# First loads of a gated attention and GEGLU kernel: one DMA queue in the order of need, wk in finer pieces, seven warm-up matmuls

## The chip, the cores and the metric

The kernel runs on one core of a Trainium2 chip. The core has five engines that run side by side, each with its own in-order stream of instructions: TensorE (PE in the profile; its weight loads are shown apart as PEld), VectorE (DVE), ScalarE (ACT), GpSimd (POOL) and SyncE (SP). They wait for each other through semaphores. Loads from device memory are issued by SP or ACT, each into a queue of its own (q1 and q10 in the profile), and moved by 16 DMA engines. The metric is the device time of one execution in microseconds (us), given as the median over several runs.

## The reference

The input x has 2048 rows of 512. Two branches are computed from it and mixed by a gate for each row. Branch a is attention with a compressive memory, 32 heads of 16, in 4 segments of 512 rows; branch b is a GEGLU feed-forward with an inner width of 1792.

```python
g = sigmoid((x * gate_w).sum(-1, keepdims=True))
# branch a, for each segment s of 4:
p = softmax(qs @ ks.T * scale + causal_mask); a_dot = p @ vs
pq = phi(qs); a_mem = (pq @ M) / (pq @ z + 1e-6)
o = sigmoid(beta) * a_mem + (1 - sigmoid(beta)) * a_dot
M = M + phi(ks).T @ vs; z = z + phi(ks).sum()
a = concat(o) @ wo
# branch b
b = (gelu(x @ w_gate) * (x @ w_up)) @ w_down
return g * a + (1 - g) * b
```

## The kernel before

The work is cut by segment s = 0 to 3. For each segment the kernel makes K and Q transposed (tasks `K{s}_t`, `Q{s}_t`, t = 0 to 3, each four matmul steps kb over the contraction), V by tiles of 128 rows (`V{s}_t`), the scores (`qk{s}_{t}{A0,B0,L,A1,B1}`, L868), their exponentials on ScalarE (`exp...`, L874), the causal masks on GpSimd (`msk...`, L877), the products with V (`pv...`, L916 and L924), the memory (`mz`, `num`), the gate and up projections of the feed-forward (`G{s}_ft`, `U{s}_ft`, ft = 0 to 13) and the last projection with `wo` and `w_down` (`D{s}_t`). Nearly all plain matmuls are recorded at L505, which is a helper.

The order on each engine is written out by hand in the table `ORDER` (L41 to L138): one list of task names for each of `pe`, `act`, `dve`, `pool` and `sp`. A name with a dot is a piece of a task: `Q0_1.2` is the part of Q0_1 that starts at contraction step 2. In segment 0 the K tasks are cut finer: each step is made in two halves of 256 rows, so that `K0_t.0` to `K0_t.3` are the steps kb = 0 to 3 of rows 0 to 255, and `K0_t.4` to `K0_t.7` those of rows 256 to 511. The class `Sched` (L207 on) walks these lists to give out the four rotating PSUM banks `psW` and the order of planning; `DMA_RATE`, `COLD`, `LANDING` and the like are its assumptions. They decide nothing else: the engines run as the lists and the semaphores have it.

The scores of one group fill `psXALL`, four banks, and ScalarE turns them into one `pt` tile (128x2048) per group. The next group of scores can't be written before that exponential has read the banks. So PE is given other work between two groups: the pieces of G, U, V, K, Q and D that stand between two `qk` names in the list. Where that work is shorter than the exponential, PE waits.

What happens first (L562 to L607):

- SP and ACT both issue loads at the start. SP issues `x0_0` and `x0_1` (rows 0 to 255 and 256 to 511 of x, 256 KB each, into the tile `hT` of the other buffer, L572), then `w_wv0`, `w_wv1` (256 KB each), `w_wg0` (896 KB), and then, mixed with the small loads `w_gwb` and `w_beta`, the four transposing loads `x1_0` to `x1_3` of segment 1 (L553), and `w_wg1`. ACT issues `w_wk0`, `w_wk1`, `w_wq0`, `w_wq1` (256 KB each); `wk{0,1}` hold the contraction steps 0-1 and 2-3.
- PE runs warm-up matmuls on a constant (L590): ten before the first real work and an eleventh, `warm10`, after the first eight transposes. They compute nothing that is used.
- When `x0_0` has landed, PE transposes rows 0 to 255 of x against an identity (L599, eight transposes into `psXALL`, tasks `x0t0a_0`, `x0t0b_0`, `x0t1_0`); DVE and ACT copy them to the tile `xT` (L607, L606, tasks `x0ev...`); then K of the first half is made, step by step.
- On ScalarE the activation table is loaded by the first activation, `tload` (L567), which stands behind the four loads that ACT issues.
- GpSimd makes the identity, masks (L609 to L613), small constants (L621, L622) and then fills the V tiles (L616, L618).

From the score group `qk0_0A0` on, the attention of segment 0 runs, with V0, Q1, K1, V1 and the G tasks of segments 0 and 1 as the work between the groups. In the list of before the first task that reads segment 1 of x is `G1_1.0`, just ahead of `qk0_0B0`.

Of the kernel before, what the change touches and what calls it, by code (L numbers as in the profile page):

```python
# [32 lines left out]
COLD = 4.9  # L33
# [4 lines left out]
    "w_wk0": 4.8, "x0_0": 4.4, "w_wk1": 6.2, "x0_1": 5.8, "w_wq0": 8.2, "w_wv0": 7.4, "w_wq1": 10.1, "w_wv1": 8.9,  # L38
    "w_wg0": 11.5, "x1_0": 12.1, "w_gwb": 12.4, "x1_1": 13.0, "w_beta": 13.3, "x1_2": 13.8, "x1_3": 14.3,
# [39 lines left out]
        "U3_9.0 U3_9.2 U2_2.0 U2_2.2 U3_8.0 U3_7.0 qk3_0B0 U3_5.0 U3_10.0 U3_8.2 U3_7.2 U3_5.2 qk3_0L U3_10.2 "
        "U3_3.0 U3_3.2 U3_4.0 D2_0.0 qk3_0A1 num3_01.0 U3_4.2 D2_0.2 D2_0.4 num3_00.0 D2_0.6 num3_02.0 qk3_0B1 "  # L80
        "D2_0.8 D2_0.10 D2_1.0 D2_1.2 U3_6.0 qk3_1A0 D2_0.12 U3_2.0 D2_0.14 U3_6.2 U3_2.2 qk3_1B0 D2_0.16 D2_1.4 "
        "U3_13.0 D2_1.6 D2_1.8 qk3_1A1 num3_11.0 num3_10.0 D2_1.10 D2_1.12 D2_1.14 U3_13.2 qk3_1B1 U3_1.0 "
        "num3_12.0 D2_1.16 U3_1.2 U3_0.0 qk3_2A0 pv3_0_0 pv3_0_1 U3_0.2 D2_3.0 qk3_2B0 D2_3.2 D2_3.4 pv3_1_1 "
        "pv3_1_0 qk3_2L D2_3.6 D2_3.8 D2_3.10 D2_2.0 D2_3.12 qk3_2A1 D2_3.14 D2_2.2 D2_2.4 D2_2.6 D2_3.16 qk3_2B1 "
        "D3_1.0 D2_2.8 D2_2.10 U3_12.0 U3_12.2 qk3_3A0 D3_1.2 D2_2.12 U3_11.0 D3_1.4 D2_2.14 qk3_3B0 U3_11.2 "
        "D3_0.0 D3_1.6 D2_2.16 D3_0.2 qk3_3A1 pv3_2_0 pv3_2_1 D3_1.8 D3_0.4 qk3_3B1 D3_0.6 D3_1.10 D3_0.8 D3_1.12 "
        "D3_0.10 D3_3w1.0 pv3_3_0 pv3_3_1 D3_3w0.0 D3_0.12 D3_2.0 D3_2.2 D3_0.14 D3_2.4 D3_2.6 D3_1.14 D3_0.16 "
        "D3_1.16 D3_3w1.4 D3_3w1.8 D3_3w0.4 D3_3w1.12 D3_3a1.0 D3_2.8 D3_2.10 D3_2.12 D3_2.14 D3_2.16 D3_3w0.8 "
        "D3_3w0.12 D3_3a0.0 "),
    "act": (  # L90
        "w_wk0 w_wk1 w_wq0 w_wq1 tload x0ev0b_0 x0ev1_0 K0_1ev K0_0even pke0_0 Q0_1ev Q0_0ev Q0_3ev gexp Vev0_1 "
        "exp0_0A0 Vev0_3 Vev0_0 exp0_0B0 gsum0_1 exp0_0L Gev1_1 exp0_0A1 gexs0 Gev0_3 exp0_0B1 pke0_1 exp0_1A0 "
        "Gev1_0 exp0_1B0 Q1_0ev exp0_1A1 pqe1_0 Gev1_9 exp0_1B1 K1_1ev Gev0_9 exp0_2A0 K1_2ev exp0_2B0 pqe1_1 "
        "exp0_2L K1_3ev exp0_2A1 Gev1_12 exp0_2B1 gsum1_0 exp0_3A0 Vev1_3 exp0_3B0 Gev1_3 exp0_3A1 Gev0_12 gexs1 "
        "exp0_3B1 gelu0_0 Gev1_13 gelu0_2 gelu0_6 gelu0_10 gelu1_0 gelu1_7 exp1_0A0 kl1_01 exp1_0B0 exp1_0L "
        "Q2_1ev exp1_0A1 exp1_0B1 pke1_0 exp1_1A0 pke1_1 exp1_1B0 fin0_0 exp1_1A1 pqe2_0 exp1_1B1 fin0_2 exp1_2A0 "
        "K2_0ev exp1_2B0 pqe2_1 exp1_2L exp1_2A1 exp1_2B1 gsum2_0 exp1_3A0 gsum2_2 exp1_3B0 gexs2 Q3_1ev exp1_3A1 "
        "K2_2ev exp1_3B1 gelu2_0 gelu2_1 gelu2_2 gelu2_3 gelu2_4 gelu2_5 gelu2_6 gelu2_7 gelu2_8 gelu2_9 gelu2_10 "
        "gelu2_11 gelu2_12 gelu2_13 exp2_0A0 exp2_0B0 pke2_0 exp2_0L exp2_0A1 pke2_1 exp2_0B1 fin1_0 exp2_1A0 "
        "Q3_3ev exp2_1B0 fin1_2 exp2_1A1 exp2_1B1 Vev3_0 exp2_2A0 exp2_2B0 pqe3_0 exp2_2L exp2_2A1 K3_3ev "  # L100
        "exp2_2B1 exp2_3A0 exp2_3B0 gsum3_3 gexs3 exp2_3A1 pqe3_1 exp2_3B1 gelu3_0 gelu3_1 gelu3_2 gelu3_3 "
        "gelu3_4 gelu3_5 gelu3_6 gelu3_7 gelu3_8 gelu3_9 gelu3_10 gelu3_11 gelu3_12 gelu3_13 exp3_0A0 exp3_0B0 "
        "exp3_0L exp3_0A1 exp3_0B1 exp3_1A0 exp3_1B0 exp3_1A1 exp3_1B1 exp3_2A0 exp3_2B0 exp3_2L exp3_2A1 "
        "exp3_2B1 fin2_3 exp3_3A0 exp3_3B0 exp3_3A1 exp3_3B1 fin3_0 fin3_1 fin3_2 fin3_30 "),
# [1079 lines left out]
```

## Time and profile before

| | us |
|---|---|
| median of 3 runs | 266.92 (266.64 to 267.32) |
| time of the profiled execution | 267.31 |
| its span, first to last instruction | 265.6 |
| PE busy in it | 261.7 |
| DVE, ACT, POOL busy | 201.2, 209.8, 109.0 |

The profile is of one execution. Its span is from the first to the last instruction; the time of the same execution is 1.7 us longer. TensorE is the busiest engine by far, and the table of slices on the page shows it busy in nine tenths or more of every slice but the first and the last.

### The profile page before, as it was taken

The page shows a single profiled execution, that of the slowest core. Times are in us where ns is not written, and L with a number is a line of the kernel's source. Part 1 is how long each engine was busy: PE and PEld are TensorE (multiplying, and loading weights), DVE is VectorE, ACT ScalarE, POOL GpSimd, SP SyncE. Part 2 cuts the span into 40 slices and gives each one's busy share as a digit, 9 for nine tenths or more (in the row PEclk, how much of TensorE's full clock was granted, in tenths as well). Part 3 has the DMA queues.
Part 4 walks back from the last instruction along what each step waited for, and adds up shares of the span by engine and source line. Part 5 has one row for each costly group of instructions (what it writes and reads, how often), then busy time and mean ns, then how long its engine had stood idle before and what let it go on. Part 6 is the DMA issues. An engine that isn't in the chain of part 4 may idle for free.

```text
span 265.6 us, 7154 instructions
## 1 busy us (share of the span) xinstructions
PE 261.7 (99%) x3021; PEld 119.5 (45%) x3021; DVE 201.2 (76%) x399; ACT 209.8 (79%) x182; POOL 109.0 (41%) x256
## 2 busy tenths in 40 slices
PE   8999999999999999999999999999999999999995
PEld 3644345434445444534444444544444444444452
DVE  0589988989889897858987875886895965892650
ACT  3589998999997899979948798887977767768611
POOL 8305857075400483372560137416184056245400
PEclk9999999999999999999999999999999999999999
DMA  6960357905102443750000246200000202201002
GB/s 213 308 173 0 63 133 131 225 17 158 61 0 47 136 62 81 151 70 22 0 2 2 47 110 106 83 2 22 1 2 0 46 0 62 62 0 42 22 12 69
DMA packets 32752, 18.23 MB, mean 69 GB/s; under 512 B 20560, under 2 KB 32720, under 8 KB 32720
## 3 DMA queue, kind: packets, MB, share of 16 engines
q1 hardware_dynamic: 31632, 16.73, 27.4%
q10 hardware_dynamic: 1088, 1.05, 1.2%
q8 instruction: 23, 0.38, 0.6%
q14 instruction: 9, 0.07, 0.1%
HBM read 9.84 MB, written 2.10 MB: 45 GB/s over the span
## 4 chain that ended last, share of the span: by engine, by line
PE 96%; DMA 2%; ACT 1%; issue 0%; ACTq 0%
PE psW L505 76%; PE psXALL L868 9%; PE psW L916 6%; PE psXALL L505 3%; DMA hT<-in_A_x_dram 2%; PE psW L924 1%; PE psW L836 1%; ACT pt L874 1%; PE psXALL L599 0%; ACT ost L1044 0%; PE psW L590 0%; ACTq L401 0%
## 5 line engine op out<-in xcount | busy, mean ns | idle before, releaser
L874 ACT ACTIVATE pt<-psXALL 128x2048 bf16<-128x2048 f32 x64 | 120.1, 1876 | 23.3 <-PE psXALL L868 21.2
L877 POOL TENSOR_SCALAR_AFFINE_SELECT pt<-pt 128x256 bf16<-128x256 bf16 x128 | 57.5, 460 | 72.1 <-ACT pt L874 67.2
L505 PE MATMUL psW<-xT,wu 128*128 128x512 bf16 x224 | 56.0, 380 | 0.0
L505 PE MATMUL psW<-wd,hT 128*128 128x512 bf16 x210 | 55.2, 380 | 0.0
L505 PE MATMUL psW<-xT,wg 128*128 128x512 bf16 x224 | 53.4, 380 | 0.0
L877 POOL TENSOR_SCALAR_AFFINE_SELECT ptl<-ptl 128x512 bf16<-128x512 bf16 x32 | 23.9, 746 | 65.5 <-ACT ptl L874 63.8
L1015 DVE TENSOR_TENSOR hT<-psW,hT 128x512 bf16<-128x512 f32 x56 | 37.0, 682 | 14.3 <-PE psW L505 13.9
L505 PEld LDWEIGHTS psW<-xT,wg 128*128 128x128 bf16 x224 | 20.8, 98 | 25.7 <-issue 1.9
L505 PEld LDWEIGHTS psW<-xT,wu 128*128 128x128 bf16 x224 | 20.5, 98 | 24.7 <-issue 1.5
L930 DVE STREAM_TRANSPOSE tb<-psW 128x512 f32<-128x512 f32 x32 | 21.7, 701 | 9.0 <-PE psW L924 8.9
L505 PEld LDWEIGHTS psW<-wd,hT 128*128 128x128 bf16 x210 | 18.6, 98 | 21.6 <-issue 3.2
L868 PE MATMUL psXALL<-qT,kpad 32*128 32x320 bf16 (+3 forms) x512 | 25.4, 273 | 0.1
L999 ACT ACTIVATE hT<-psW 128x512 bf16<-128x512 f32 x28 | 15.4, 596 | 7.2 <-PE psW L505 7.1
L916 PE MATMUL psW<-pt,vaug 128*17 128x192 bf16 (+3 forms) x512 | 18.8, 273 | 0.0
L868 PEld LDWEIGHTS psXALL<-qT,kpad 32*128 32x128 bf16 x512 | 7.6, 92 | 23.9 <-ACT pt L874 14.2
L779 POOL COPY exsT<-exs 32x4 f32<-32x4 f32 x64 | 16.7, 261 | 3.7
L505 PE MATMUL psW<-wv,xT 128*128 128x512 bf16 x64 | 18.2, 380 | 0.0
L505 PE MATMUL psW<-xT,wk 128*128 128x512 bf16 (+1 forms) x80 | 18.0, 337 | 0.0
L874 ACT ACTIVATE ptl<-psXALL 128x2048 bf16<-128x2048 f32 x8 | 15.0, 1876 | 3.4 <-PE psXALL L868 3.4
L505 PE MATMUL psW<-wo,oT 128*128 128x512 bf16 x60 | 16.5, 381 | 0.0
L522 DVE CAST hT<-psW 128x512 bf16<-128x512 f32 x19 | 12.6, 682 | 2.2 <-PE psW L505 2.1
L916 PEld LDWEIGHTS psW<-pt,vaug 128*17 128x17 bf16 x512 | 10.6, 91 | 7.9 <-issue 3.2
(102 smaller groups left out, 311.2 us busy)
## 6 DMA issues: line engine op xcount, KB each, us to landing
out_dram<-ost SPq DMA_DIRECT2D x15, 128.0 KB, 1.7
wg<-in_B_w_gate_dram SPq DMA_DIRECT2D x2, 896.0 KB, 7.3
wu<-in_B_w_up_dram SPq DMA_DIRECT2D x2, 896.0 KB, 6.7
wd<-in_B_w_down_dram SPq DMA_DIRECT2D x2, 896.0 KB, 5.6
phkt<-in_A_x_dram SPq DMA_DIRECT2D x3, 512.0 KB, 5.4
vlow<-vaug SPq DMA_DIRECT2D x8, 136.0 KB, 2.7
hT<-in_A_x_dram SPq DMA_DIRECT2D x2, 256.0 KB, 4.7
wk<-in_A_wk_dram ACTq DMA_DIRECT2D x2, 256.0 KB, 5.1
```

Of the source, the lines that this page charges most:

```text
L505: return Instr(lambda e: e.matmul(view(), lhsT, rhs, start=first, stop=last), reads=reads, writes=[fkey if fkey is not None else g.key], e ...
L522: alts[DVE] = [Instr(lambda e: e.tensor_copy(dst(), src()), reads=reads, writes=writes, est=dve_t(n))]
L779: cross = task(f"exsT{s}", POOL, [Instr(lambda e, g=g, c=c: e.tensor_copy(exsT[sl][32 * g:32 * g + 32, c:16:4], exs[32 * c:32 * c + 32, s4 ...
L836: Instr(lambda e, t=t, kt=kt, c=c: e.matmul(gm.f32()[32 * c:32 * c + 32, 34 * t:34 * t + 34].rearrange("p (j e) -> p j e", e=17), phkt[:, ...
L868: instrs.append(Instr(lambda e, g=g, lhs=lhs, rhs=rhs, c0=c0, ncol=ncol: e.matmul(X[g][:, c0:c0 + ncol], lhs(32 * g), rhs(32 * g), start=T ...
L874: exp_task(s, f"exp{s}_{t}{name}", [Instr(lambda e: e.activation(dst[:], XALL[:, :].rearrange("p (g c) -> p g c", g=4), ACTF.Exp, scale=AT ...
L877: task(f"msk{s}_{t}{name}", POOL, [Instr(lambda e, view=view, pat=pat, base=base: e.affine_select(out=view, in_=view, compare_op=ALU.is_ge ...
L916: instrs.append(Instr(lambda e, t=t, q=q, kb=kb, slot=slot, c0=c0: e.matmul(gp.f32()[32 * q:32 * q + 17, 128 * kb + 64:512], Vaug[sl][:, k ...
L924: instrs.append(Instr(lambda e, t=t, q=q, kb=kb, c0=c0: e.matmul(gp.f32()[32 * q:32 * q + 17, 128 * kb:128 * kb + 64], Vlow[j][:, kb, 4 * ...
L930: task(f"pvt{s}_{t}_{j}", DVE, [Instr(lambda e: e.transpose(Tb[:, j, :], gp.f32()[:, :]), [gp.key], [("Tb", j)], dve_t(512))], grp=gp)
L999: lambda e, g=g, ft=ft, s=s: e.activation(hT[s % 2][:, ft, :], g.f32()[:, :], ACTF.Gelu_apprx_tanh),
L1015: task(f"Um{s}_{ft}", DVE, [Instr(lambda e, g=g, ft=ft: e.tensor_tensor(hT[sl][:, ft, :], g.f32()[:, :], hT[sl][:, ft, :], ALU.mult), [g.k ...
```

## The change

The loads of x0, wk, wq and wv all go to SP's queue, in the order x0_0, wk0, x0_1, wk1, wk2, wq0, wq1, wv0, wv1; ACT issues none. `wk` is loaded in three pieces instead of two: step 0 (128 KB), step 1 (128 KB) and steps 2-3 (256 KB), and K0's steps wait for the piece that they read. The warm-up matmuls are seven instead of eleven (six of 512 columns, the last of 256), all of them ahead of the first transposes. The scheduler's assumptions are changed, and all five lists are written anew: besides the first part, the pieces between the score groups stand in another order through all four segments. The sets of tasks are the same but for the loads of wk and the warm-ups. On ScalarE the first instruction is now the table load, ahead of the wait of the first copy `x0ev0b_0`; on GpSimd the V tiles are filled before the small constants.

```diff
-COLD = 4.9
+COLD = 4.4
 LANDING = {
-    "w_wk0": 4.8, "x0_0": 4.4, "w_wk1": 6.2, "x0_1": 5.8, "w_wq0": 8.2, "w_wv0": 7.4, "w_wq1": 10.1, "w_wv1": 8.9,
-    "w_wg0": 11.5, "x1_0": 12.1, "w_gwb": 12.4, "x1_1": 13.0, "w_beta": 13.3, "x1_2": 13.8, "x1_3": 14.3,
+    "x0_0": 3.8, "w_wk0": 4.2, "x0_1": 4.9, "w_wk1": 5.2, "w_wk2": 5.9, "w_wq0": 6.6, "w_wq1": 7.3, "w_wv0": 8.0,
+    "w_wv1": 8.7, "w_wg0": 11.2, "x1_0": 11.8, "w_gwb": 12.1, "x1_1": 12.8, "w_beta": 13.1, "x1_2": 13.6, "x1_3": 14.2,
 }
 ORDER = {
     "pe": (
-        "warm0 warm1 warm2 warm3 warm4 warm5 warm6 warm7 warm8 warm9 x0t0a_0 x0t0b_0 x0t1_0 warm10 K0_0.0 K0_1.0 "
-        "K0_2.0 K0_3.0 K0_0.1 K0_1.1 K0_2.1 K0_3.1 x0t0_1 x0t1_1 K0_0.2 K0_0.3 K0_2.2 K0_3.2 K0_2.3 K0_3.3 K0_1.2 "
...
+        "warm0 warm1 warm2 warm3 warm4 warm5 warm6 x0t0a_0 x0t0b_0 x0t1_0 K0_1.0 K0_0.0 K0_3.0 K0_2.0 x0t0_1 "
+        "K0_0.1 K0_3.1 K0_2.1 K0_1.1 x0t1_1 K0_2.2 K0_1.2 K0_3.2 K0_2.3 K0_3.3 K0_1.3 K0_0.2 K0_1.4 K0_0.3 K0_0.4 "
+        "K0_2.4 K0_1.5 K0_0.5 K0_1.6 K0_0.6 K0_1.7 Q0_3.0 K0_3.4 K0_0.7 Q0_3.2 K0_2.5 Q0_2.0 K0_2.6 Q0_1.0 Q0_1.2 "
+        "K0_3.5 Q0_0.0 K0_3.6 Q0_2.2 K0_2.7 Q0_0.2 V0_1.0 V0_0.0 K0_3.7 V0_1.2 qk0_0A0 G0_1.0 Q1_2.0 Q1_2.2 "
+        "G0_1.2 V0_0.2 V0_3.0 qk0_0B0 G0_6.0 V0_3.2 V0_2.0 V0_2.2 G1_5.0 qk0_0L G1_5.2 G0_2.0 Q1_3.0 G0_2.2 "
...
-        "D2_0.8 D2_0.10 D2_1.0 D2_1.2 U3_6.0 qk3_1A0 D2_0.12 U3_2.0 D2_0.14 U3_6.2 U3_2.2 qk3_1B0 D2_0.16 D2_1.4 "
-        "U3_13.0 D2_1.6 D2_1.8 qk3_1A1 num3_11.0 num3_10.0 D2_1.10 D2_1.12 D2_1.14 U3_13.2 qk3_1B1 U3_1.0 "
-        "num3_12.0 D2_1.16 U3_1.2 U3_0.0 qk3_2A0 pv3_0_0 pv3_0_1 U3_0.2 D2_3.0 qk3_2B0 D2_3.2 D2_3.4 pv3_1_1 "
+        "D2_0.14 D2_1.2 qk3_1B0 D2_1.4 D2_0.16 U3_0.0 U3_6.0 U3_0.2 qk3_1A1 U3_6.2 num3_11.0 D2_1.6 D2_1.8 "
+        "num3_10.0 U3_1.0 qk3_1B1 D2_1.10 D2_1.12 D2_1.14 D2_1.16 num3_12.0 U3_1.2 qk3_2A0 D2_3.0 U3_13.0 U3_13.2 "
+        "D2_3.2 pv3_0_0 qk3_2B0 pv3_0_1 pv3_1_0 pv3_1_1 D2_2.0 qk3_2L D2_2.2 D2_2.4 D2_3.4 D2_2.6 D2_3.6 qk3_2A1 "
...
     "act": (
-        "w_wk0 w_wk1 w_wq0 w_wq1 tload x0ev0b_0 x0ev1_0 K0_1ev K0_0even pke0_0 Q0_1ev Q0_0ev Q0_3ev gexp Vev0_1 "
+        "x0ev0b_0 tload x0ev1_1 K0_1ev K0_0even K0_0ev pke0_0 Q0_3ev Q0_2ev Q0_0ev K0_2ev gexp exp0_0A0 kl0_30 "
...
     "dve": (
-        "x0ev0a_0 x0ev0_1 x0ev1_1 kl0_11 K0_0ev kp0_1 K0_2ev Q0_2ev kl0_10 kl0_01 gmul0 gsum0_0 K0_3ev kl0_21 "
+        "x0ev0a_0 x0ev1_0 x0ev0_1 kl0_10 kp0_0 kl0_11 Q0_1ev kp0_1 kl0_01 K0_3ev Vev0_1 gmul0 Q1_2ev Vev0_0 "
...
     "pool": (
-        "ident masks consts vones msk0_0L exsT0 msk0_0B0 msk0_0A1 msk0_0A0 msk0_1A0 msk0_0B1 msk0_1B0 omg "
+        "ident masks vones msk0_0A0 msk0_0A1 omg msk0_0L msk0_0B1 msk0_1A0 msk0_0B0 consts exsT0 msk0_1B0 "
...
     "sp": (
-        "x0_0 x0_1 w_wv0 w_wv1 w_wg0 x1_0 w_gwb x1_1 w_beta x1_2 x1_3 w_wg1 pkT0_1 Vlo0_0 pkT0_0 Vlo0_1 pkT0_2 "
+        "x0_0 w_wk0 x0_1 w_wk1 w_wk2 w_wq0 w_wq1 w_wv0 w_wv1 w_wg0 x1_0 w_gwb x1_1 w_beta x1_2 x1_3 w_wg1 Vlo0_0 "
...
-                avail = max(t.finish + 3.0, LANDING[t.name])
+                avail = max(t.finish + 2.3, LANDING[t.name])
...
+    wloads = [(wkey, i, w[:, k0:k1, :], r4(src)[:, k0:k1, :])
+              for wkey, w, src, cuts in (("wk", wk, A_wk, (0, 1, 2, 4)), ("wq", wq, A_wq, (0, 2, 4)),
+                                         ("wv", wv, A_wv, (0, 2, 4)))
+              for i, (k0, k1) in enumerate(zip(cuts, cuts[1:]))]
     for u in range(2):
         rank[0] -= 20000.0
         dma(f"x0_{u}", SP, lambda u=u: xin[:, 2 * u:2 * u + 2, :],
             lambda u=u: A_x[0, u * 256:(u + 1) * 256, :].rearrange("(a p) d -> p a d", p=P), [],
-            [("hT", 1, 2 * u + a) for a in range(2)], (230000, 300000)[u], bias=rank[0], issue=0.45)
-        wdma(("wk", u), ACT, wk[:, 2 * u:2 * u + 2, :], r4(A_wk)[:, 2 * u:2 * u + 2, :], (220000, 310000)[u], issue=0.45)
-    for key, w, src, e in (("wq", wq, A_wq, ACT), ("wv", wv, A_wv, SP)):
-        for i in range(2):
-            wdma((key, i), e, w[:, 2 * i:2 * i + 2, :], r4(src)[:, 2 * i:2 * i + 2, :], 250000, issue=0.46)
+            [("hT", 1, 2 * u + a) for a in range(2)], 250000, bias=rank[0], issue=0.5)
+        for wkey, i, dst, src in wloads[u:u + 1] if u == 0 else wloads[1:]:
+            wdma((wkey, i), SP, dst, src, 250000, issue=0.5)
...
-    for i in range(11):
+    for i in range(7):
         gw = Grp(banks)
-        n = 384 if i in (6, 9, 10) else 512
+        n = 256 if i == 6 else 512
...
-        wk_of = lambda kb: ("w", (wkey, kb // 2))
+        wk_of = lambda kb: ("w", (wkey, min(kb, 2) if wkey == "wk" else kb // 2))
```

## The prediction

> **What bounds the kernel now.** I read the page first (busy shares, then the chain of work that ended last), then the order of time of the first 16 us, then the rates of the DMA queues and the chain near 226 us.
>
> ```profile
> PE 261.7 (99%) x3021; PEld 119.5 (45%) x3021; DVE 201.2 (76%) x399; ACT 209.8 (79%) x182; POOL 109.0 (41%) x256
> PE 96%; DMA 2%; ACT 1%; issue 0%; ACTq 0%
> ```
>
> PE is busy for 99% and is 96% of the chain. The rest of the chain is the first load (DMA 2%) and one stretch of ACT. So only three things can move the end: when PE's first useful work starts, at which clock it runs, and whether PE waits later.
>
> ```profile
> 0.81 0.97 SPq L536 DMA_DIRECT2D hT<-in_A_x_dram  x2
> 0.81 1.03 ACTq L536 DMA_DIRECT2D wk<-in_A_wk_dram  x2
> 0.84 4.21 PE L590 MATMUL psW<-const-bfloat16-1.0 128*128 128x512 bf16 x10 [0.84 <-PEq L1169]
> 2.91 1.28 ACT L567 ACT_TABLE_LOAD   x1 [2.91 <-issue]
> 2.93 0.15 PEld L590 LDWEIGHTS psW<-const-bfloat16-1.0 128*128 128x128 bf16 x1 [0.28 <-issue]
> 3.36 0.15 PEld L590 LDWEIGHTS psW<-const-bfloat16-1.0 128*128 128x128 bf16 x1 [0.28 <-issue]
> 3.44 2.13 SPq L532 DMA_TRANSPOSE xT<-in_A_x_dram  x1
> 5.10 0.76 PE L599 MATMUL psXALL<-ident,hT 128*128 128x128 bf16 x8
> 5.54 0.29 DVE L607 COPY xT<-psXALL 128x256 bf16<-128x256 bf16 x1 [5.54 <-PE psXALL L599]
> 5.88 1.05 PE L505 MATMUL psW<-xT,wk 128*128 128x256 bf16 x8
> 6.23 1.32 SPq L532 DMA_TRANSPOSE xT<-in_A_x_dram  x1
> 7.60 1.29 SPq L536 DMA_DIRECT2D betab<-in_A_beta_dram  x1
> 8.94 4.23 SPq L532 DMA_TRANSPOSE xT<-in_A_x_dram  x2
> 10.91 1.89 PE L505 MATMUL psXALL<-xT,wq 128*128 128x512 bf16 x8
> ```
>
> Up to 5.05 PE runs warm-ups; x0_0 lands at 5.06 (0.81 + 4.25 in the chain) and the transposes start 0.04 later. From there PE has no gap to speak of. The warm-ups' weight loads are 0.43 apart for 512 columns, while eight later 512-column matmuls start 0.216 apart (1.89 less the last one's drain): PE starts at half speed. Within the eight transposes of 5.10 the starts go from 0.107 apart to 0.055 at about 5.43, so full speed comes there, 4.6 us after the first warm-up. (The page's clock row has no record before that point and prints full speed.)
>
> ```profile
> 3.90:8.50 4.60, 4.55 (x40) 3.19 (x39) 1.05 (x3) 1.37 (x4) 4.60 (x4) 1.00 1.09 358
> 64.00:66.00 2.00, 2.00 (x10) 0.77 (x8) 1.93 (x6) 1.97 (x3) 1.43 (x6) 1.00 1.09 385
> wo<-in_A_wo_dram SPq DMA_DIRECT2D x1, 512.0 KB, 4.0
> 225.79 0.44 PE psXALL L868 x8
> 226.25 1.89 ACT pt L874
> 228.18 0.40 PE psXALL L868 x8
> ```
>
> The last number of the first two rows is GB/s: two queues together move 358 in the head, one queue alone 385 later, with packets of 1 KB too. The last three rows are the one place where PE waits for an exponential.
>
> **The change, part by part.** *First load.* x0_0 no longer shares the engines with wk0. Nearest row: wo, 512 KB on SP's queue, lands 4.0 after its issue; its second 262 KB take 262/385 = 0.68, so a first 256 KB takes about 3.3 and lands at 0.81 + 3.3 = 4.1. Upper bound: the 5.06 of now (no gain). I take 4.2, near the row that is like it.
>
> *Head of PE.* Transposes start at 4.24. At half speed eight take 8 x 0.107 = 0.86; the copy path needs 5.88 - 5.10 = 0.78 from first transpose to first K0 matmul, so the transposes decide: K0 starts at 5.10 instead of 5.88, 0.78 sooner. With full speed still at 5.43, 0.33 of it runs at half speed and loses 0.17. **Net 0.61.** If full speed came before 4.24, K0 would start at 4.24 + 0.78 = 5.02: 0.86. The removed warm-ups give nothing by themselves: ten lay in the wait for x0_0, the eleventh (0.16 of PE) in the wait for the copy.
>
> *Later pieces.* Behind x0_0 each 256 KB lands 0.68 apart (262/385), each 128 KB 0.34: wk0 4.54, x0_1 5.22, wk1 5.56, wk2 6.24, wq0 6.9, wq1 7.6, wv1 9.0. PE asks for x0_1 at 5.10 + 0.44 + 0.17 = 5.71, wk1 at 5.93, wk2 at 6.59, wq0 at 6.59 + 16 x 0.109 = 8.3. Smallest margin 0.35, so no wait; at 358 GB/s wk2 is at 6.4, still in time. The sixth to ninth issue (0.5 each) stay ahead of the data.
>
> *Issues.* SP now issues nine loads before wg0 instead of four: five more at 0.51, so x1_0 could be issued at 6.0 instead of 3.44, and gwb, beta, x1_1 to x1_3 and wg1 behind it. What waits: PE's `Q1_2.0` (x1_0, x1_1) and `Q1_2.2` (x1_2, x1_3), moved up to just after `qk0_0A0`, and ScalarE's `gexp` (beta). PE gets to Q1_2.0 after 32 K0 (3.49), 8 transposes (0.45), 16 Q0 (3.45), 6 V0 (1.29), the scores (0.43) and 2 G0 (0.43): 5.10 + 0.17 + 9.54 = 14.8, and to Q1_2.2 at 15.2. In the trace of before x1_3's issue ends at 13.17 and it lands at 14.86. Bounds: SP's row has waits in it (2.13, 1.29 and 2.93 for issues that take 1.26, 0.57 and 1.26 where the queue is free: 3.3 too long). Without them the row ends at 12.3 in spite of five more issues and x1_3 lands near 14.0; with all of them it lands at 14.86 + 2.55 = 17.4. I take 14.9, since the bytes ahead of x1 are the same in sum and the engines drain them at the same rate: no wait.
>
> *Table load.* 1.28 of ACT, from 2.91 to 0.81. It is done long before the first copy either way: nothing. Were it behind that copy's wait, it would cost up to 1.28. *GpSimd.* Its V fill (3.77 + 1.96) moves 0.9 up, the constants back; V's first copy comes near 12.6: nothing.
>
> *Later order.* The PE work is the same in sum. Between `qk3_1B1` and `qk3_2A0` the old list has 8 matmuls of 0.216 and 2 of 0.057 = 1.84; the scores and this take 2.17, but the rows above show 2.46 from one group's start to the next (225.72 to 228.18): PE waits 0.29. The new list has 10 and 2 there (2.27), 2.60 with the scores, more than the 2.46 that the exponential needs. **Gain 0.29.** Every other stretch between score groups has at least 2.06 in the new list, which the old one also has at places with no wait, so I take no new wait; bounds 0 and one missed exponential of 0.3 to 0.6.
>
> Sum: 0.61 + 0.29 = 0.90. The profiled execution's 267.31 would become 266.4 (span 265.6 to 264.7); it lies 0.39 over the median, which becomes 266.92 - 0.90 = **266.0**.
>
> **The rivals.** *B, the first load lands no sooner.* For: from 1.8 to 2.8 us the engines move only 14 and then 117 GB/s, so the start is slow before any sharing counts. Against: wo. Only the later 0.29 stays: 266.6.
>
> *C, the pause keeps PE slow.* Seven warm-ups end at 0.84 + 6 x 0.427 + 0.213 = 3.6 (3.8 drained), and PE then idles till 4.24. Before, PE had one pause of 0.05 in its 4.6 us of slow work. If full speed needs such work without a pause, and the count starts again at 4.24, it comes at 4.24 + 4.6 = 8.84 instead of 5.43: 3.41 at half speed cost 1.70, so 267.7. For: the fall at the end of the trace shows that idling brings the slow clock back:
>
> ```profile
> 262.70:265.58 2.88, 0.00 (x0) 0.00 (x0) 0.00 (x0) 0.58 (x1) 0.00 (x0) 0.87 0.24 80
> ```
>
> A mean clock of 0.87 over 2.88 us without matmuls is full speed for 2.1 and half for the rest. Against: that took over 2 us of idling, this pause is 0.45. The Trainium skill's page "TensorE: Matmul & The Clock Gate" (Part 1, The HAM clock gate) says that a free-running window of about 3.4 us decides, and advises 4 us of warm-up matmuls; the change has 2.8, which speaks against it. 5.43 and the fall near 264.85 are indeed 76 such windows apart. By that rule the window that ends at 5.43 would be about four fifths busy, and what share suffices no row here shows.
>
> *D, the loads of x1 come late (the other side).* If SP's row moves back by its whole 2.55, x1_3 lands at 17.4 and PE stands at Q1_2.2 from 15.2 on: 2.2 lost one for one, 268.2. It costs something from a landing at 15.2, outweighs the gain from 16.1. For: before, nothing read x1 before about 17.3, so the margin shrinks from 2.4 to 0.3. Against: the waits in SP's row.
>
> **How the numbers follow.** A (forecast) 0.62: 266.0, its own range 265.5 to 266.4. B 0.10, C 0.12, D 0.16. About 0.8 us, 0.3%, is what a measurement of this kernel can tell from no change, so faster means under 266.12. From A 0.50 faster, 0.12 same; B gives 0.10 same; C lies at the bound, 0.09 slower, 0.03 same; D 0.14 slower, 0.01 same and 0.01 faster where the delay is small. Faster 0.51, same 0.26, slower 0.23. Low end: x0_0 at 4.1 and full speed at once, 0.95 + 0.29 = 1.24, and 0.3 that runs vary: 265.3. High end: past C, and D with most of its delay: 267.9.
>
> **What would show it.** Right: first L599 at 4.1 to 4.5, first K0 near 5.1, no second slow stretch after 5.5, PE's gap before `qk3_2A0` gone, PE's last end 0.9 sooner. B: L599 at 4.7 or later. C: K0 matmuls of 256 columns 0.21 apart past 6 us. D: a gap of PE ahead of Q1_2 ended by a DMA of xT. The prediction is wrong if PE waits anywhere after 18 us where it did not before.

## The result and the profile after

The changed kernel takes 268.24 us (median of 17 runs, 267.88 to 269.66); the kernel before, run beside it, 267.32 (17 runs, 266.63 to 268.23). The ratio is 1.0043, with a 95% interval of 1.0028 to 1.0058: slower by 0.92 us by the medians and 1.15 by the ratio, where 0.9 us faster was predicted. The profiled execution of after took 269.1 us (span 267.3), one of its slower ones; the median of its spans is 266.4. Where a single execution can mislead, the medians of the experiments decide below.

The page of after, busy times and the chain of work that ended last:

```profile
PE 256.3 (96%) x2980; PEld 118.2 (44%) x3017; DVE 200.2 (75%) x396; ACT 209.9 (79%) x186; POOL 105.7 (40%) x256
...
PE 89%; DVE 4%; DMA 3%; issue 2%; SPq 1%; ACT 0%; ACTq 0%; DVEq 0%
```

PE's busy time can't be compared with the 261.7 of before: the work is the same but for the warm-ups, and some matmul records are missing (2980 beside 3017 weight loads, one of which goes with each matmul). The chain can: PE falls from 96% to 89%, and loads and DVE, which were 2% and absent, stand in it with 3% and 4%. So PE now waits, and for two kinds of thing.

The first is the loads. The order of time of PE at the start (start, length, engine, line, what, number, and in brackets the idle time before it and what ended it):

```profile
3.72 0.76 PE L600 MATMUL psXALL<-ident,hT 128*128 128x128 bf16 x8
4.50 0.61 PE L504 MATMUL psW<-xT,wk 128*128 128x256 bf16 x4
5.51 0.40 PE L600 MATMUL psXALL<-ident,hT 128*128 128x128 bf16 x4 [0.40 <-DMA hT<-in_A_x_dram]
...
7.58 1.91 PE L504 MATMUL psW<-xT,wk 128*128 128x256 bf16 x16 [0.79 <-DMA wk<-in_A_wk_dram]
...
10.80 0.38 PE L504 MATMUL psXALL<-xT,wq 128*128 128x512 bf16 x1 [0.67 <-DMA wq<-in_A_wq_dram]
```

The first transposes start 1.38 us sooner than before (3.72 against 5.10), and so does K0 (4.50 against 5.88). Then PE stands still three times, 0.40 + 0.79 + 0.67 = 1.86 us, for x0_1, for wk2 and for wq1: more than was won. Each of these waits costs more than the gap that is shown, since the matmul ahead of it is listed with its drain (0.38 us for 512 columns, where matmuls that follow each other start 0.216 apart). The first score group starts at 15.66 instead of 14.57, with 0.11 us more work ahead of it in the new list: 0.98 late. From K0's first matmul to there it takes 2.36 us longer than before for the same work, 1.38 of which the early start had won. The windows say why:

```profile
3.90:8.50 4.60, 3.33 (x33) 2.42 (x32) 1.14 (x3) 1.07 (x3) 4.14 (x4) 1.00 0.92 272
```

In the same window two queues moved 358 GB/s before; now the one queue moves 272.

The second is near 60 us. The chain there (start, length, what):

```profile
53.84 1.74 PE psW L504 x8
55.58 0.02 issue
55.60 0.69 DVE hT L521
56.30 0.52 DVE mzbd L851
...
56.84 0.70 DVE mzbd L851
...
57.57 0.71 DVE mzbd L851
...
58.30 0.70 DVE mzbd L851
58.99 0.03 issue
59.02 1.28 DVE glog L768 x2
60.30 0.61 DVE vaug L521
60.92 0.05 issue
60.96 1.04 PE psW L504 x4
```

For 5.3 us DVE carries the chain. PE waits (0.64 us idle before 60.96) for a PSUM bank that the copy Vev1_0 (tile vaug) frees, and in DVE's new list this copy stands behind mzbd0 and two sums. In the list of before mzbd0 stands behind Vev1_0 and all of DVE's sums. At the same place before, DVE was:

```profile
55.59 1.27 DVE L767 TENSOR_REDUCE glog<-phkt 128x1 f32<-128x512 bf16 x2
56.77 0.68 DVE L522 CAST hT<-psW 128x512 bf16<-128x512 f32 x1
57.37 1.85 DVE L850 TENSOR_TENSOR mzbd<-mzacc,gbd 32x136 bf16<-32x136 f32 x4
```

One thing went as meant. Of the two score groups near 226 us the chain of after reads:

```profile
226.81 0.33 PE psXALL L869 x8
227.14 0.16 issue
227.30 2.22 PE psW L504 x11
229.52 0.33 PE psXALL L869 x8
```

The exponential that stood between them in the chain of before is gone. To add such things up I set the start of every score group against the work that stands ahead of it in PE's list, and take the difference between the kernels. It is +0.98 us at the first group and stays within about 0.1 until `qk0_3A1`, where it steps to +1.88; it stays there within 0.1 until `qk3_2A0`, where it falls by 0.18, and PE's last matmul ends 1.67 later (264.37 against 262.70). Two places lose, one gains, and all else is as it was.

### The profile page after: what moved, and what is told of

Read it like the earlier page. It is cut to its first block, busy times and chain, and to the rows that moved or that the text cites. A ratio compares the mean times of both kernels' runs of the same rounds, so it can differ in the third digit from the quotient of the medians.

```text
span 267.3 us, 7109 instructions
## 1 busy us (share of the span) xinstructions
PE 256.3 (96%) x2980; PEld 118.2 (44%) x3017; DVE 200.2 (75%) x396; ACT 209.9 (79%) x186; POOL 105.7 (40%) x256
## 4 chain that ended last, share of the span: by engine, by line
PE 89%; DVE 4%; DMA 3%; issue 2%; SPq 1%; ACT 0%; ACTq 0%; DVEq 0%
PE psW L504 72%; PE psXALL L869 8%; PE psW L917 5%; PE psXALL L504 3%; DMA wq<-in_A_wq_dram 3%; PE psW L925 1%; SPq L535 1%; DVE mzbd L851 1%; DVE tb L931 1%; DVE hT L1016 0%; DVE glog L768 0%; DVE ost L1065 0%; DVE hT L521 0%; PE psW L837 0%; DVE vaug L521 0%
## 5 line engine op out<-in xcount | busy, mean ns | idle before, releaser
L504 PE MATMUL psW<-xT,wu 128*128 128x512 bf16 x216 | 54.4, 380 | 0.8 <-issue 0.3
L504 PE MATMUL psW<-xT,wg 128*128 128x512 bf16 x217 | 52.3, 379 | 1.6 <-DVE vaug L521 0.8
L504 PE MATMUL psW<-wd,hT 128*128 128x512 bf16 x196 | 52.0, 380 | 1.9 <-issue 1.7
L878 POOL TENSOR_SCALAR_AFFINE_SELECT ptl<-ptl 128x512 bf16<-128x512 bf16 x32 | 22.3, 696 | 46.4 <-ACT ptl L875 44.7
L780 POOL COPY exsT<-exs 32x4 f32<-32x4 f32 x64 | 14.7, 230 | 3.8 <-ACT exs L771 0.2
L521 DVE CAST hT<-psW 128x512 bf16<-128x512 f32 x20 | 13.5, 686 | 3.4 <-PE psW L504 3.3
```

Source lines behind the costliest of these rows:

```text
L504: return Instr(lambda e: e.matmul(view(), lhsT, rhs, start=first, stop=last), reads=reads, writes=[fkey if fkey is not None else g.key], e ...
L521: alts[DVE] = [Instr(lambda e: e.tensor_copy(dst(), src()), reads=reads, writes=writes, est=dve_t(n))]
L780: cross = task(f"exsT{s}", POOL, [Instr(lambda e, g=g, c=c: e.tensor_copy(exsT[sl][32 * g:32 * g + 32, c:16:4], exs[32 * c:32 * c + 32, s4 ...
L878: task(f"msk{s}_{t}{name}", POOL, [Instr(lambda e, view=view, pat=pat, base=base: e.affine_select(out=view, in_=view, compare_op=ALU.is_ge ...
```

## The experiments

Two theories at first. **Q:** one queue moves the early loads more slowly than two, and the loads come late. **M:** the wait near 60 us is DVE's order, mzbd0 ahead of Vev1_0. Each run has its own ratio to before, run beside it on the same chip. Landings and the time at which the clock comes to full are read from the profiled executions.

**e1, wk and wq on ScalarE's queue again, the rest as after.**

```diff
-            wdma((wkey, i), SP, dst, src, 250000, issue=0.5)
+            wdma((wkey, i), SP if wkey == "wv" else ACT, dst, src, 250000, issue=0.5)
```

> The kernel after, with only the five loads of wk and wq issued by ACT again (q10), ahead of the table load; pieces, order, warm-ups and all else as after. Theory Q (one queue moves the early loads at 272 GB/s where two moved 358, so the later pieces, wg0 and the row of segment 1 come 2 us late): wk2 lands by 7.0 instead of 7.44, wg0 by 12.5 instead of 14.44, x1_3 by 15.2 instead of 16.91; x0_0 lands later than 3.67 because wk shares the engines; the head loses some 0.3 us instead of 0.98 against before and the time is 267.6, 0.6 under after. Rival R (the rate is set by the small pieces or by the memory, not by the number of queues): the same bytes land at the same times as in after, wg0 14.4, x1_3 16.9, time 268.2. Theory M (the wait near 60 us is DVE's order, mzbd0 ahead of the copy Vev1_0): that wait, 0.64 us of PE, stays in either case.

Measured: 268.86 us, ratio 1.0058 (1.0044 to 1.0072), 0.47 over after on the same chip (268.39, e4 below): no gain. wk2 landed at 6.53 and x1_3 at 14.58 as Q has it, but wq1 only at 10.15, behind wv0 and wv1 on the other queue, and PE waited 1.21 us for it. The rate rose; what matters is which load it serves.

**e2, the kernel before with wk and wq moved to SP's queue, in two pieces each, nothing else.**

> The kernel before, with only the four loads of wk and wq moved to SP, in the order x0_0 wk0 x0_1 wk1 wq0 wq1 wv0 wv1; eleven warm-ups, two pieces of wk and all orders of before. Theory Q: x0_0 lands near 3.7, wg0 near 14.4 and x1_3 near 16.9, PE gains nothing at the start since its ten warm-ups run to 5.1, and the time is 0.5 to 1.0 us over before (267.8 to 268.3). Rival R (pieces of 128 KB cost the rate): wg0 by 12.5 and x1_3 by 15.2, time as before within 0.2 (267.3).

Measured: 267.86, ratio 1.0018 (1.0006 to 1.0031). The time is near Q's, but the profiled execution (its fastest run, 267.13) had neither landing: wg0 at 12.01, x1_3 at 14.63, 331 GB/s from 3.90 to 8.50. By this one execution R looked right. By the median the move to one queue, with nothing else changed, costs 0.4 to 0.5 us.

**e3, after with mzbd0 later in DVE's list.**

```diff
-... Gev0_13 mzbd0 gsum1_0 gsum1_3 Vev1_0 gsum1_2 Q2_0ev Gev1_8 Gev0_0
+... Gev0_13 gsum1_0 gsum1_3 Vev1_0 gsum1_2 Q2_0ev Gev1_8 mzbd0 Gev0_0
```

> The kernel after, with only mzbd0 moved in DVE's list from ahead of gsum1_0 to behind Gev1_8, so that the copy Vev1_0, which frees a PSUM bank, no longer stands behind it. Theory M: PE's wait of 0.64 us near 60.3 us is gone and the time is 0.8 under after, 267.4. Rival (the wait is of that one execution, or another takes its place within the next group): 268.2, as after.

Measured: 267.61, ratio 1.0006 (0.9996 to 1.0017). **e4, after unchanged**, on the same chip: 268.39, ratio 1.0035 (1.0018 to 1.0051).

> The kernel after, unchanged, for a second profile and beside the others on the same chip. Theory Q and theory M: the landings are the same within 0.3 (wk2 7.4, wq1 10.5, wg0 14.4, x1_3 16.9) and PE waits again near 60 us; time 268.2. Rival (stalls of that one execution): the landings or the wait near 60 us differ by over 0.5 us.

So 0.78 us of the loss is this one name in one list. In the second profile of after PE waits 0.65 at the same place, and the landings differ by at most 0.6 (wk2 6.88, wq1 10.35, wg0 14.21, x1_3 16.63). In e3 the wait is gone: the eight matmuls ahead of the score group run in one piece.

```profile
59.01 1.89 PE L504 MATMUL psW<-xT,wg 128*128 128x512 bf16 x8
60.83 0.40 PE L869 MATMUL psXALL<-qT,kpad 32*128 32x448 bf16 x8
```

**e8, after with GpSimd's mask on ptl moved, DVE's list untouched.**

```diff
-... msk0_2B1 msk0_2L msk0_3A0 msk0_3B0
+... msk0_2B1 msk0_3A0 msk0_2L msk0_3B0
```

> The kernel after, DVE's list untouched, with GpSimd's mask msk0_2L (2.8 us on the tile ptl) moved behind msk0_3A0 in its list, so that it no longer runs beside mzbd0. Theory M2 (mzbd0 is slow, 0.69 us a piece, because GpSimd works at the same time, and so the copy behind it is late): the four pieces of mzbd0 take 1.0 to 1.5 us instead of 2.78, PE's wait of 0.65 near 60.8 us falls under 0.1, and the time is 0.6 to 0.8 under after: 267.6. Rival (mzbd0 is slow by itself, and only the order counts): the pieces stay at 0.69, the wait stays, time 268.3.

Measured: 267.34, ratio 1.0005 (0.9991 to 1.0019), the same as e3's. The order of time of DVE in e8:

```profile
54.56 0.69 DVE L521 CAST hT<-psW 128x512 bf16<-128x512 f32 x1 [0.17 <-PE psW L504]
55.17 1.26 DVE L851 TENSOR_TENSOR mzbd<-mzacc,gbd 32x136 bf16<-32x136 f32 x4
56.46 1.28 DVE L768 TENSOR_REDUCE glog<-phkt 128x1 f32<-128x512 bf16 x2
57.65 0.68 DVE L521 CAST vaug<-psW 128x512 bf16<-128x512 f32 x1
```

and of GpSimd in e8:

```profile
54.12 0.90 POOL L878 TENSOR_SCALAR_AFFINE_SELECT pt<-pt 128x256 bf16<-128x256 bf16 x2 [1.84 <-ACT pt L875]
56.93 0.90 POOL L878 TENSOR_SCALAR_AFFINE_SELECT pt<-pt 128x256 bf16<-128x256 bf16 x2 [1.91 <-ACT pt L875]
57.78 2.84 POOL L878 TENSOR_SCALAR_AFFINE_SELECT ptl<-ptl 128x512 bf16<-128x512 bf16 x4
```

The same mask in after:

```profile
56.01 2.83 POOL L878 TENSOR_SCALAR_AFFINE_SELECT ptl<-ptl 128x512 bf16<-128x512 bf16 x4
```

The four pieces of mzbd0 take 1.26 us while GpSimd is idle, and took 2.8 in after (56.22 to 58.99), where the mask ran from 56.01 to 58.84. Vev1_0 is still behind them and comes in time. The wait needs both: the order, and the mask beside it. The Trainium skill ("SBUF — State Buffer", SBUF: two separate sides) says that a DVE operation with two SBUF inputs and a GpSimd operation that reads SBUF exclude each other for a whole instruction; the trace agrees: four pieces of mzbd0 in 2.78 us beside four of the mask in 2.83.

**Back to the loads. e5: e3 with the early loads on two queues in the order of need.**

```diff
-            wdma((wkey, i), SP, dst, src, 250000, issue=0.5)
+            wdma((wkey, i), ACT if wkey == "wk" or (wkey, i) == ("wq", 1) else SP, dst, src, 250000, issue=0.5)
```

> The kernel after with mzbd0 later in DVE's list (as in e3) and the early loads on two queues in the order of need: ACT issues wk0, wk1, wk2 and wq1, SP x0_0, x0_1, wq0, wv0, wv1, wg0. Theory Q2 (one queue stalls on single packets between 2.8 and 8 us, two don't, and e1 lost only because wq1 stood behind wv0, wv1 on the other queue): no packet over 0.12 us between 4.5 and 8 us, x0_0 lands by 4.4, wk2 by 6.6, wq1 by 8.8, PE waits for no load after K0 starts but x0_1 (under 0.2 us); the head ends 0.4 to 0.6 us sooner than before and the time is 266.7, 0.9 under e3. Rival P (the early start of PE is worth nothing, since PE runs at half clock or waits for later loads anyway): time as e3, 267.5.

Measured: 266.93, ratio 1.0006 (0.9989 to 1.0024). Ten runs of twelve lie from 266.81 to 267.25, two at 268.50 and 268.99, and these two bring the ratio over 1. x0_0 landed at 4.35, wk2 6.56, wq1 8.44; no wait for a load after K0's start; the first score group 0.40 sooner than before for the same work. Against the before of the same chip (267.10) the median is 0.17 under, where e3's was 0.13 over (267.48): 0.3 gained on e3, not 0.9.

**e6, e3 with wk in two pieces of 256 KB, on the one queue.**

> The kernel after with mzbd0 later and wk again in two pieces of 256 KB, all still on SP's queue in the order x0_0 wk0 x0_1 wk1 wq0 wq1 wv0 wv1. Theory S (the pieces of 128 KB are what costs the one queue its rate, as e2 against e3 and e4 suggests): wk1 lands near 6.7, wq1 near 8.1, wv1 near 9.4, x1_3 near 14.6, no wait of PE over 0.3 us in the head, time 0.5 under e3: 267.1. Rival V (the late landings are chance from run to run, with two pieces as with three): wq1 anywhere from 8 to 10.5, time as e3 within 0.2: 267.6.

Measured: 267.59, ratio 1.0022 (1.0005 to 1.0039); wk1 landed at 7.96, wq1 at 9.43, wv1 at 10.93, and PE waited 1.1 for x0_1 and 0.8 for wk1. The size of the pieces is not the cause: S fell, and the good landings of e2 were one execution's.

**e7, e3 with eleven warm-ups ahead of the transposes.**

> The kernel after with mzbd0 later and eleven warm-ups with the widths of before, all ahead of the first transposes, so that these start near 5.3 us instead of 3.7. Theory P (the early start is worth nothing while wk2, x0_1 and wq1 come as late as they do): wk2 and wq1 end PE's waits as before, and the time is as e3 within 0.2: 267.6. Rival (the early start does carry to the end): 0.6 to 1.2 over e3, 268.3 to 268.8.

Measured: 267.53, ratio 1.0021 (1.0008 to 1.0035). In its profile the clock came to full at 3.49, so the warm-ups were over sooner than expected: PE started its transposes at 4.35, 0.63 later than in after, and still waited 1.2 for wk2. Its ratio is 0.15%, 0.4 us, over e3's, between the two theories and with intervals that overlap: while the loads come as they do, little of the 1.38 us by which after starts sooner is left.

**The pause. e9: e5 with nine warm-ups that end where x0_0 lands; e10: e5 with five, which end near 3.0.**

> The kernel e5 (two queues in the order of need, mzbd0 later) with nine warm-ups instead of seven (eight of 512 columns, the last of 256), so that they run to about 4.4 us, where x0_0 lands, and the pause of 0.62 us before the first transposes is gone. Theory C (the two runs of e5 at 268.5 and 269.0 are executions whose clock window met the pause and kept TensorE at half speed for one window of 3.4 us more): no run over 267.6, median 266.8, and a ratio to before under 1 by 0.001 to 0.002. Rival (those two runs have another cause, a late load): again one run in six 1.5 us over the median, median 266.9.

> The kernel e5 with five warm-ups of 512 columns instead of seven, so that they end near 3.0 us and the pause before the first transposes is 1.4 us. Theory C: fewer windows are busy enough, the clock comes to full between 5 and 8.5 us, and the times spread from 266.9 to 269 with a median 0.5 to 1.2 over e5: 267.4 to 268.1. Rival (the clock comes with the first window after the start whatever the pause, or the loads hide a slow start): median as e5, 266.9.

Measured: e9 267.03, ratio 1.0000 (0.9988 to 1.0013), twelve runs from 266.73 to 267.85: no run near 268.5, but neither the gain nor the bound of 267.6 that C had for it. e10 268.10, ratio 1.0049 (1.0031 to 1.0067), eight runs from 267.85 to 269.25; its clock came to full at 8.14 us, and both are as C has them. PE in e10, order of time:

```profile
4.35 1.03 PE L600 MATMUL psXALL<-ident,hT 128*128 128x128 bf16 x8 [1.21 <-DMA hT<-in_A_x_dram]
5.18 1.06 PE L504 MATMUL psW<-xT,wk 128*128 128x256 bf16 x4
```

and in e11, below, where it came to full at 4.07:

```profile
4.96 1.05 PE L504 MATMUL psW<-xT,wk 128*128 128x256 bf16 x8
```

Four matmuls in the time of eight: half speed. A pause of 1.2 us costs 1.1 us (e10 against e9). That e5's two late runs were such executions is likely and not shown (no profile fell on one); the kernels with two queues and a pause (e5, e13) have four of 24 runs over 268, those without (e9, e11) none of 24. The kernel before, which has hardly a pause, has eight of 155 over 268 itself, so other causes are not ruled out.

**The head alone. e12: the kernel before with only the changed head** (loads, pieces, warm-ups, table load); **e11: the same with e9's two queues and nine warm-ups.**

> The kernel before with all its later orders, and only the head of e9: wk in three pieces, ACT issues wk0, wk1, wk2, wq1, SP x0_0, x0_1, wq0, wv0, wv1, and nine warm-ups that end at 4.4 us, all ahead of the transposes. Theory H (with two queues in the order of need and no pause the early start is kept): x0_0 lands near 4.4, K0 starts near 5.15 instead of 5.88, no wait for a load after it over 0.2 us, the first score group starts 0.4 to 0.6 sooner than before's 14.57, and the time is 0.4 to 0.5 under before: ratio 0.998 to 0.9985. Rival (the gain is taken back at the row of segment 1 or by the finer loads): ratio 1.000 within 0.001.

> The kernel before with all its later orders, and only the head of the change: all nine early loads on SP in the order of need, wk in three pieces, seven warm-ups ahead of the transposes, table load first on ScalarE. Theory Q (one queue's stalls of single packets take the early start back): the landings spread as in after (wk2 6.9 to 7.8, wv1 10.5 to 12.0, x1_3 15.4 to 16.9), the first score group starts 0 to 1.0 later than before's 14.57, the wait near 60 us is not there, and the time is 0.1 to 0.6 over before: ratio 1.0005 to 1.0025. Rival (the stalls come from after's other order of work): ratio under 1, as e11.

Measured: e12 267.84, ratio 1.0035 (1.0015 to 1.0055); e11 266.97, ratio 0.9999 (0.9983 to 1.0015). The window from 3.90 to 8.50 us (length, busy time of PE, its weight loads, DVE, ACT and GpSimd with their numbers, clock, share and GB/s of the DMA engines), first e12, then e11:

```profile
3.90:8.50 4.60, 3.31 (x33) 2.67 (x32) 1.05 (x3) 0.98 (x2) 4.60 (x4) 1.00 0.88 293
```

```profile
3.90:8.50 4.60, 4.44 (x45) 3.48 (x44) 1.05 (x3) 1.62 (x5) 4.60 (x4) 1.00 1.10 358
```

In the same 4.6 us PE runs 45 matmuls with two queues and 33 with one. What waits in e12 (us in total, times, longest):

```profile
PE psW L504 <- DMA wk<-in_A_wk_dram: 1.3, 2, 1.0
```

So the changed head alone makes before slower. With two queues it does not, but the gain that the profile of e11 shows (first score group 0.65 sooner, one of its two fastest runs, 266.67) is not in the median: H fell as to the time. e12 lost more than Q had (0.7 us by the median, where 0.1 to 0.6 was expected), though wv1 and x1_3 landed a little sooner than Q's ranges.

**e13: e12 with wk1, wk2 and wq1 on ScalarE's queue, and the table load still first; e14: before again.** In all kernels with one queue so far the table load came at 0.8 us, in all with two at about 3, so the two had to be told apart.

> The kernel e12 (before's later orders, wk in three pieces, seven warm-ups, table load first on ScalarE) with wk1, wk2 and wq1 issued by ACT, behind the table load; SP keeps x0_0, wk0, x0_1, wq0, wv0, wv1. Theory Q (the stalls are the single queue's): no packet over 0.12 us between 4.5 and 8 us, x0_0 still lands near 3.6 and wk0 near 3.9, wk2 by 6.6, wv1 by 9.5, K0 starts at 4.45 and the time is 0.3 to 0.6 under e12's and 0 to 0.4 under before. Rival T (the early table load stalls the early loads): long packets between 2.8 and 8 us as in e12, landings of wk2 after 7 and of wv1 after 10, time as e12, ratio 1.002 to 1.005.

> The kernel before, unchanged, for a second profile. Theory C (the clock comes to full between 3.5 and 6.9 us by the phase of its window, and that spreads the times): landings within 0.3 us of the first profile's (x0_0 5.06, wk0 5.39, wq1 10.42, x1_3 14.86), the first score group at 14.57 less half of the time by which the clock comes sooner than 5.44, or later by half of what it comes later. Rival (the landings spread in before too): x0_0 or wq1 differ by over 0.5 us.

Measured: e13 267.19, ratio 1.0005 (0.9987 to 1.0023); the table load ran from 0.80 to 2.08, ACT's first issue at 0.86 beside it, 360 GB/s from 3.90 to 8.50, and no packet between 2.8 and 8 us took over 0.12 us. T fell: e13 differs from e12 in the queue of three loads alone, and it is 0.65 us faster on the same chip.

```profile
0.80 1.28 ACT L566 ACT_TABLE_LOAD   x1 [0.80 <-PEq L1170]
0.86 0.94 ACTq L535 DMA_DIRECT2D wk<-in_A_wk_dram  x2
3.90:8.50 4.60, 3.62 (x37) 3.11 (x38) 1.05 (x3) 0.91 (x2) 4.60 (x4) 1.00 1.11 360
```

x0_0 and wk0 landed at 4.24 and 4.64, later than Q had them. PE waited 0.6 us for x0_1, which stood third on its queue. e14 took 267.26, with its clock full at 5.62 and the first score group at 14.51: the profile of before is a fair one, though x0_0 (4.71) and wk0 (5.02) landed 0.35 sooner in it.

Landings in the profiled executions, us:

| | queues | x0_0 | x0_1 | last of wk | wq1 | wv1 | x1_3 |
|---|---|---|---|---|---|---|---|
| before | 2 | 5.06 | 6.46 | 6.89 | 10.42 | 9.58 | 14.86 |
| after | 1 | 3.67 | 5.46 | 7.44 | 10.53 | 11.99 | 16.91 |
| e12 | 1 | 3.54 | 5.60 | 7.37 | 8.69 | 10.14 | 15.23 |
| e11 | 2 | 4.24 | 5.37 | 6.43 | 8.15 | 9.13 | 14.35 |
| e13 | 2 | 4.24 | 6.67 | 5.28 | 6.85 | 9.03 | 14.24 |

**e15: e11 with the late wait before `qk3_2A0` filled.**

```diff
-... U3_0.0 qk3_2A0 pv3_0_0 pv3_0_1 U3_0.2 D2_3.0 qk3_2B0 D2_3.2 ...
+... U3_0.0 U3_0.2 qk3_2A0 pv3_0_0 pv3_0_1 D2_3.0 D2_3.2 qk3_2B0 ...
```

> The kernel e11 (before's later orders, early loads on two queues in the order of need, wk in three pieces, nine warm-ups), and in PE's list of segment 3 the pieces from qk3_1B1 on drawn one place forward, so that U3_0.2 stands ahead of qk3_2A0 and each later stretch keeps its length. If the wait of 0.29 us before qk3_2A0 is the only one there, the span falls by 0.2 to 0.3 under e11's median of 265.2 and the time is 266.7, ratio to before 0.998 to 0.9990. Rival (the wait moves to the last group, where one piece less stands between qk3_3B1 and pv3_3): as e11, 267.0, ratio 0.9995 to 1.0005.

Measured: 268.05, ratio 1.0033 (1.0019 to 1.0048): a miss, and in neither of the two ways expected. PE in e15:

```profile
228.09 0.40 PE L869 MATMUL psXALL<-qT,kpad 32*128 32x448 bf16 x8
...
230.28 0.81 PE L504 MATMUL psW<-wo,oT 128*128 128x512 bf16 x3 [0.57 <-DVE tb L931]
```

The score group follows its predecessor (225.38) after 2.71 us of pure work instead of 2.46 with the wait in it (the same 2.46 in e11), and then the next piece waits 0.57 for DVE, whose own list was left as it was. A further 0.29 goes to an exponential ahead of a piece at 251.56. A piece drawn forward on PE needs its bank sooner. No version that I ran beats before; e3, e5, e8, e9, e11 and e13 can't be told from it.

## Why the prediction was wrong, point by point

**First load and head of PE.** Right in kind, too small in size. x0_0 was put at 4.2 with 4.1 as the lower bound; it landed at 3.67, and K0 started at 4.50, not 5.10. The wo row set the bound too high. Full speed, taken at 5.43, came at 4.04 in one profile of after and at 6.84 in the other: not a property of the kernel but of the execution.

**Later pieces. This step failed.** It took 262 KB each 0.68 us behind x0_0 and found "smallest margin 0.35, so no wait", with 358 GB/s as the careful case. The 385 came from a load at 65 us, the 358 from two queues; no row showed one queue in the first 8 us. There x0_1 landed 0.24 later than put, wk2 1.20 and wq1 2.9, and three margins were gone. The gain of 0.61 became nothing or a loss: in the new lists about +0.2 (e3's median span is 265.75 against 265.6; the late stretch takes 0.18 off it, and small stalls in segment 0 of up to 0.2 are in it), in the old lists +0.7 (e12). Why the old lists lose more is open. With two queues in the order of need the same head costs nothing (e11, e9), and in the profiled executions PE starts K0 at 5.0 to 5.2 and keeps that to the end, which the medians of e9 and e11 don't show.

**No new wait in the later order. This step failed too.** It looked at the length of each stretch against the exponential and set "0 and one missed exponential of 0.3 to 0.6". The wait that came is for a PSUM bank, through DVE's list, which was never read. It cost 0.78 (e4 against e3), and it was there to be found: the changed list has mzbd0 ahead of Vev1_0, and the trace of before has pieces of mzbd from 0.25 to 0.69 us.

**Gain before `qk3_2A0`.** Right, 0.18 instead of 0.29. It was added as free; e15 shows that the same step in another list is not.

**Issues and rival D.** x1_0 was issued at 5.84 (6.0 predicted) and x1_3 landed at 16.91, inside the bounds of 14.0 to 17.4 but far from the 14.9 taken. PE did not wait for it: the list of its waits up to 20 us names x0_1, wk2, wq1 and one DVE copy of 0.2 (a weight load waited 0.20 for it, and the matmuls still followed 0.216 apart). It came to Q1_2 at 16.43, late enough itself. So D's time, 268.2, was met by luck and D was not the cause. But the 14.9 was wrong by 2.0 and only didn't show because PE was late itself: at 15.2, where the prediction had PE at Q1_2.2, it would have waited 1.7 us. (The lower bounds in that paragraph add up to 12.4 and 14.1, not 12.3 and 14.0.) Only ScalarE's gexp waited 0.80 for beta, and no group of scores came later for it.

**Rival C.** A pause does cost, and C's price was near (e10: 1.1 us for a pause of 1.2, where C had 1.70), but not by a count that starts again: e5, with a pause of 0.62, came to full speed at 5.78, 1.39 us after its transposes started. And in after x0_0 lands as the warm-ups end, so there was hardly a pause. The Trainium skill ("TensorE: Matmul & The Clock Gate", Part 1, The HAM clock gate) has a free-running window of about 3.4 us decide the clock; the traces agree, with 3.413, and bound the share that suffices (below). The same page (Why this matters for your kernels) advises 4 us of warm-up matmuls; with 2.9 us of them, and work right behind, after came to full speed at 4.04 and 6.84, and before, with ten of them in 4.2 us, at 5.44 and 5.62.

**Rival B** fell (x0_0 came 1.4 sooner). **Table load and GpSimd's fill** cost nothing, as predicted; no wait names them.

The sum: 0.90 faster was forecast and 0.92 slower came, 1.82 apart. The head is about 0.8 of it, DVE's order 0.8, the smaller gain 0.1. The last 0.1 lies outside the span: time less span is 1.85 us in the median of after (17 runs) and 1.83 to 1.87 in every kernel with its lists, and 1.70 to 1.76 in e2, e11, e12, e13 and before itself. e15, which differs from e11 only in PE's list from 225 us on, has 1.85 as well, so it comes with the order of the end; how is open.

## What to carry to other kernels

A rate is worth what its row is like: take the one of the same stage with the same number of queues, and before moving loads to one queue look at whether the two of now run at once. When an order is written anew, read the list of every engine that frees a buffer, not only the length of the work between two waits; a slow small operation ahead of a copy cost 0.78 us here, more than the 0.3 to 0.6 that the prediction allowed for a missed exponential. Work drawn forward on one engine has to be drawn forward on those that empty its banks as well.

## What the runs showed of the hardware

- **One queue moves less than two in the first microseconds, and stalls on single packets.** From 3.90 to 8.50 us the eight profiles with one queue (after, e2, e3, e4, e6, e7, e8, e12) show 272 to 331 GB/s, the nine with two (before in both profiles, e1, e5, e9, e10, e11, e13, e15) 357 to 363. In the packet records each of the eight has between 7 and 13 packets of 1 KB that took 0.12 to 1.7 us from 4.5 to 6 us, while the usual one takes about 0.05; the nine have none from 4.5 to 8 us. Sooner than that two queues are not free of them: before has 8 and 9, of up to 0.50 us, from 2.8 to 4.5 us. After 8.5 us one queue is as fast as two were: 374 GB/s from 8.50 to 12.00 in after. Issuing is not what is short: wk2, issued at 2.80 in after, landed at 7.44, and wv1, issued at 4.81, at 11.99. What stalls the packets is open; neither the size of the pieces (e6) nor the early table load (e13) does. The Trainium skill ("DMA: Bandwidth & Descriptors", Issuing engines are not separate DMA queues) has a second issuing engine save only the time to issue; here it also gave 358 GB/s instead of 293 (e11, e12), and the measurement decides.
- **The clock's windows.** From the start of full speed to its end it is 259.413 or 262.826 us in each of the 15 profiles that record both: 76 or 77 times their difference, 3.413 us, with a phase that differs from run to run. A window with warm-ups in its last 2.59 us of 3.41 (76%) was not enough (e4, full at 6.84), one with 2.65 (78%) was (e7, full at 3.49); each is one execution. With seven warm-ups on one queue full speed came anywhere from 3.58 (e8) to 6.84 (e4).
- **DVE beside GpSimd.** A piece of mzbd of 32x136 took 0.70 us while a mask ran on GpSimd (after) and 0.32 while it was idle (1.26 for four, e8). A copy of 128x512 from PSUM took 0.69 with masks beside it (57.91 in e3, the mask from 55.73 to 58.57) and 0.68 without (52.87 in before).
- **ScalarE issues loads while it loads its table.** In e13 the table load runs from 0.80 to 2.08 and three loads are issued from 0.86 to 2.32.
